# Byte offsets for the operands of the two MLP layers: weights at 0 modulo 128, activations at eight places

## The chip, the cores and the metric

The kernel runs on one core of a Trainium2 chip. The metric is the device time of one execution in microseconds (us). An engine here is one of PE (TensorE: matmuls, with its weight loads shown as PEld), DVE (VectorE), ACT (ScalarE), POOL (GpSimd) and SP (the queue that issues most DMAs). SBUF is the on-chip memory that the engines read: 128 partitions, and in each partition a row of bytes. A tile's place is the byte at which it begins in every partition.

## The reference

Causal attention, then two MLP layers, all in float32:

```
scores = q @ k^T / sqrt(64), masked above the diagonal      # 2 batches, 12 heads, 448 positions, 64 per head
attn   = softmax(scores) @ v                                # -> x: 896 tokens x 768
h      = max(x @ w_in, 0);      x = (h * h) @ w_out         # layer 1: 768 -> 2048 -> 768
h      = x @ w_in2;  out = (h - tanh(h)) @ w_out2           # layer 2: 768 -> 2048 -> 768
```

## The kernel before, in words

**Attention.** The twelve pairs of heads go through a pipeline (the loop over `s`, lines 579 to 669): scores, row maxima, exponentials, transposes, product with v. Into the gaps of the later pairs the first six products of the first MLP layer are put (`early`, line 510).

**MLP.** Each layer is done in two halves of 1024 hidden units (line 678). A half has two stages. `first` (line 498) makes eight groups for each of two batches: one group is one PSUM bank `h` of 128 x 448, summed over the six chunks of x. `second` (line 546) makes six groups for each batch: one bank `o`, summed over eight hidden chunks `g`. A product of float32 numbers is made of three matmuls on a rounded high part and a low part, written in `pieces` (line 411): high weights times high activations (L417), high times low (L418), low times high (L419). Each of them loads 128 x 128 weights (the stationary operand) and streams 448 columns (the moving operand). That makes 18 matmuls in a group of `first`, 24 in one of `second`, 288 in a stage, and 2304 in all over eight stages.

**Tiles.** A chunk of x (line 90; in layer 2 it is named y, line 563) is one tile of [high or low][batch][448]. Two hidden chunks share one tile of g, [high or low][2][448], in one of eight slots; line 488 chooses the slot: batch 0 uses slots 5, 6, 0, 1 and batch 1 slots 3, 2, 4, 7, in this order. A weight unit, 768 high and 768 low numbers, lies in one of eight ring tiles (line 168). The strides inside the tiles (1792 and 3584 bytes for activations, 512 and 3072 for weights) are all multiples of 128, so every operand of a tile begins at the same place modulo 128 as the tile itself.

**Places before.** The pool puts one tile behind the other. From the built program's allocation, modulo 128 bytes: all chunks of x begin at 32, all ring tiles at 96, slots 0, 1, 2 and 7 at 64, and slots 3, 4, 5 and 6 at 96.

**Order.** The order of all work is written out in the program and fixed; weights are unpacked by DVE and ACT (lines 123 to 158) between the activations, and nothing in the MLP stages waits for a planner.

Of the kernel before, what the change touches and what calls it, by code (L numbers as in the profile page):

```python
# [9 lines left out]
F32R = mybir.dt.float32r  # L10
# [9 lines left out]
B, H, S, D = 2, 12, 448, 64  # L20
DM = H * D
DFF = 2048
P = 128
KD = DM // P
# [3 lines left out]
NPAIR = B * NP  # L28
NQ = S // D
RING = 8  # L30
UNIT = 6
UC = UNIT * P
NU = 2 * (KF + DFF * DM // (P * UC))
# [48 lines left out]
def body(ctx: ExitStack, tc: tile.TileContext, qT, kT, vL, w1, w2, w3, w4, out):  # L82
    nc = tc.nc
    sb = ctx.enter_context(tc.tile_pool(name="sb", bufs=1))
# [2 lines left out]
    ident = sb.tile([P, P], F32, name="ident")  # L87
    mask = sb.tile([P, BEFORE + S], F32, name="mask")
    abias = sb.tile([P, 1], F32, name="abias")
    x = [sb.tile([P, 2, B, S], F32R, tag=f"x{k}", name=f"x{k}") for k in range(KD)]  # L90

    def slot(i, shape, dt, name):
        return sb.tile(shape, dt, tag=f"slot{i}", name=name)
# [29 lines left out]
    def w_prep(u):  # L123
# [8 lines left out]
        def merge():  # L132
            late()
            lo, hi = st["lo"], st["hi"]
            nc.vector.scalar_tensor_tensor(out=lo, in0=hi, scalar=3, in1=lo, op0=ALU.logical_shift_left, op1=ALU.bitwise_or)  # L135
            if u >= WOVEN:
                st["w"] = ring(u)
                act_late.append(lambda: nc.scalar.copy(out=st["w"][:, 0], in_=lo.bitcast(F32)))  # L138

        def high():  # L140
            st["w"] = ring(u)
            nc.vector.tensor_copy(out=st["w"][:, 0], in_=st["lo"].bitcast(F32))
# [22 lines left out]

    def ring(u):
        taken.append(u)
        return sb.tile([P, 2, UC], F32R, tag="w", bufs=RING, name=f"w{u}")

    def room():  # L170
        i = len(taken) - RING
        return i < 0 or taken[i] < freed[0]
# [10 lines left out]
    def late():  # L183
        while act_late:
            act_late.pop(0)()

    def one():

        if todo and budget[0] > 0 and (room() or not todo[0][3]):
            take()  # L190
            return True
# [64 lines left out]
    def hbank(name):  # L256
        n = hcount[0] % 8
        hcount[0] += 1
        tag, bufs = ("s", 4) if n < 4 else ("t", 2) if n < 6 else ("oh"[n - 6], 1)
        return ps.tile([P, 512], F32, tag=tag, bufs=bufs, name=name)[:, :S]  # L260
# [147 lines left out]
    g = {}  # L408
# [13 lines left out]
    def group(*args):  # L422
        for _ in pieces(*args):
            pass

    def hi_of(dst, v):
        nc.scalar.copy(out=dst[0], in_=v)  # L427

    def lo_of(dst, v):
        nc.vector.tensor_sub(out=dst[1], in0=v, in1=dst[0])  # L430
# [52 lines left out]
    gt = {}  # L483

    def gdst(l, half, m, b):

        if m % 2 == 0:
            i = (5, 6, 0, 1, 3, 2, 4, 7)[4 * b + m // 2]
            gt[b, m // 2] = slot(i, [P, 2, 2, S], F32R, f"g{l}_{half}_{b}_{m // 2}")
        t = gt[b, m // 2]  # L490
        g[m, b] = (t[:, 0, m % 2], t[:, 1, m % 2])
        return g[m, b]
# [5 lines left out]
    def first(l, half, m, b):  # L498

        u = (2 * l + half) * 2 * HALF + m  # L500
        dst = gdst(l, half, m, b)
        h = hbank(f"h{u}_{b}")
        for _ in first_pieces(l, half, m, b, h):
            pass
        if b == 1:
            freed[0] = u + 1
        return lambda: (act1, act2)[l](h, dst)


    def early(count):  # L510
        for m in range(count):
            dst = gdst(0, 0, m, 0)
            h = ps.tile([P, 512], F32, tag="h", bufs=1, name=f"h{m}_0")[:, :S]
            for k, _ in enumerate(first_pieces(0, 0, m, 0, h)):
                if k == KD - 1:
                    done.append((h, dst))
                yield
# [28 lines left out]
    def second(l, half, m, b):  # L546
        u0 = (2 * l + half) * 2 * HALF + HALF
        o = hbank(f"o{u0}_{m}_{b}")
        group(o, lambda k: (u0 + (m * HALF + k) // UNIT, (m * HALF + k) % UNIT), HALF, lambda k: g[k, b])
        if b == 1:  # L550
            freed[0] = u0 + (m + 1) * HALF // UNIT
        if half == 0:
            if b == 0 and m % 3 == 0:
                t = sb.tile([P, 3, B, S], F32, tag=f"v{m // 3}", name=f"part{l}_{m}")
                for i in range(3):
                    part[m + i] = t[:, i]
            nc.scalar.copy(out=part[m][:, b], in_=o)  # L557
        else:
            p = part[m][:, b]
            if l == 0:  # L560
                nc.vector.tensor_add(out=p, in0=o, in1=p)
                if b == 0:
                    x[m] = sb.tile([P, 2, B, S], F32R, tag=f"x{m}", name=f"y{m}")
                hi_of((x[m][:, 0, b], x[m][:, 1, b]), p)
                late()
                one()
                lo_of((x[m][:, 0, b], x[m][:, 1, b]), p)
            else:

                cuts = 2 if (m, b) == (KD - 1, B - 1) else 1  # L570
                w = S // cuts
                for i in range(cuts):
                    c = slice(i * w, i * w + w)
                    nc.vector.tensor_add(out=p[:, c], in0=o[:, c], in1=p[:, c])
                    (nc.scalar if i < cuts - 1 else nc.sync).dma_start(out=out[m * P : m * P + P, b * S + i * w : b * S + i * w + w], in_=p[:, c])
# [3 lines left out]
    for s in range(NPAIR + 2):  # L579
        p, a = s - 1, s - 2  # L580
        ss, sp, sa = s < NPAIR, 0 <= p < NPAIR, a >= 0
        f = s - 2 >= NP
# [95 lines left out]
    for l in range(2):  # L678
        for half in range(2):
            order = [(m, b) for m in range(HALF) for b in range(B)]  # L680
            if l == 0 and half == 0:
                order = [(EARLY, 0), *((m, 1) for m in range(EARLY + 1)), *order[2 * EARLY + 2 :]]
            for m, b in order:
                budget[0] = min(budget[0], 0) + (SHARE_HIDDEN[l] if l == 1 or m < HALF - 1 else 0)
                first(l, half, m, b)()
                pump()
            flush()
            for m in range(KD):
                for b in range(B):
                    budget[0] = min(budget[0], 0) + SHARE_OUT  # L690
                    second(l, half, m, b)
                    late()
                    pump()
# [42 lines left out]
```

## Time and profile before

| | us |
|---|---|
| median of 3 runs | 548.28 (548.06 to 548.43) |
| the profiled execution | 548.39 |
| its span in the profile | 546.6 |
| PE busy in the span | 538.0 (98%) |
| DVE, ACT busy | 345.8, 327.9 |

The profiled execution lasts 1.8 us longer than its span, which begins with the first and ends with the last instruction recorded. Matmuls are pipelined: one lasts some 0.36 us in the trace, but the next begins about 0.20 us after it. So the busy time of a matmul says little; the distance from one start to the next says what a matmul costs.

### The profile page before, as it was taken

Reading aid. Unit: us, or ns where it says so; the run is one execution under the profiler, and the core shown is the slowest. Engines: PE = TensorE matmul, PEld = TensorE weight load, DVE = VectorE, ACT = ScalarE, POOL = GpSimd, SP = SyncE. Lnnn points to the kernel's source line nnn. Section 1 sums busy time; section 2 is a strip of 40 time slices with the busy share of each in tenths; the row PEclk is TensorE's granted clock in tenths of the full one; section 3 lists DMA queues with packets and bytes.
Section 4 is the critical chain, followed back from the end, with each engine's and each line's share of the span. In section 5 each row is a group of like instructions: output and inputs, shape, how many; then the busy total and the mean of one; then the engine's idle time right before and its main releaser. Section 6 shows DMA issues by size and latency. Waiting matters only on the chain.

```text
span 546.6 us, 8248 instructions
## 1 busy us (share of the span) xinstructions
PE 538.0 (98%) x3206; PEld 483.6 (88%) x3206; DVE 345.8 (63%) x730; ACT 327.9 (60%) x630; POOL 4.2 (1%) x21
## 2 busy tenths in 40 slices
PE   8999999999999999999999999999999999999997
PEld 4668888899999999999999999999999999999996
DVE  5999998464624154444554688997654588887311
ACT  5999987577424266665232388776543687854100
POOL 1000000000000000000000000000000000000000
PEclk9999999999999999999999999999999999999999
DMA  8744323253433333331324130113655301026111
GB/s 296 268 150 131 113 80 106 105 174 115 163 128 116 115 117 116 115 116 58 116 83 149 58 117 1 59 58 113 231 176 174 113 5 58 1 71 212 50 52 50
DMA packets 15526, 61.86 MB, mean 113 GB/s; under 512 B 1664, under 2 KB 6400, under 8 KB 15488
## 3 DMA queue, kind: packets, MB, share of 16 engines
q1 hardware_dynamic: 15200, 61.00, 33.1%
q8 instruction: 25, 0.41, 0.3%
q10 hardware_dynamic: 288, 0.34, 0.2%
q14 instruction: 13, 0.11, 0.1%
HBM read 58.59 MB, written 2.75 MB: 112 GB/s over the span
## 4 chain that ended last, share of the span: by engine, by line
PE 92%; ACT 4%; DVE 3%; issue 0%; DVEq 0%; POOLq 0%; ACTq 0%
PE o L419 14%; PE o L418 14%; PE o L417 14%; PE h L417 14%; PE h L419 14%; PE h L418 14%; PE o L369 3%; ACT p L322 2%; PE t L357 2%; PE s L289 2%; DVE p L304 1%; DVE p L343 1%; ACT pt L364 1%; PE warm L238 1%; ACT raw L121 0%; DVE x L405 0%
## 5 line engine op out<-in xcount | busy, mean ns | idle before, releaser
L419 PE MATMUL o<-g,w 128*128 128x448 f32 x384 | 140.9, 367 | 0.0
L418 PE MATMUL o<-g,w 128*128 128x448 f32 x384 | 140.7, 366 | 0.0
L417 PE MATMUL o<-g,w 128*128 128x448 f32 x384 | 140.6, 366 | 0.0
L418 PEld LDWEIGHTS o<-g,w 128*128 128x128 f32 x384 | 72.1, 188 | 6.5
L419 PEld LDWEIGHTS o<-g,w 128*128 128x128 f32 x384 | 72.1, 188 | 6.4
L417 PEld LDWEIGHTS o<-g,w 128*128 128x128 f32 x384 | 72.1, 188 | 6.3
L417 PE MATMUL h<-x,w 128*128 128x448 f32 x192 | 71.5, 372 | 0.0
L417 PE MATMUL h<-y,w 128*128 128x448 f32 x192 | 69.7, 363 | 0.0
L419 PE MATMUL h<-y,w 128*128 128x448 f32 x192 | 69.6, 362 | 0.0
L419 PE MATMUL h<-x,w 128*128 128x448 f32 x192 | 69.5, 362 | 0.0
L418 PE MATMUL h<-x,w 128*128 128x448 f32 x192 | 69.4, 362 | 0.0
L418 PE MATMUL h<-y,w 128*128 128x448 f32 x192 | 69.1, 360 | 0.0
L138 ACT CAST w<-raw 128x768 fp32r<-128x768 f32 x56 | 50.4, 900 | 26.7 <-DVE raw L135 26.7
L135 DVE SCALAR_TENSOR_TENSOR raw<-raw 128x768 int32<-128x768 int32 x64 | 61.0, 953 | 5.4 <-ACT raw L121 5.4
L121 ACT ACTIVATE raw<-raw 128x768 f32<-128x768 f32 x64 | 58.8, 918 | 0.0
L151 DVE TENSOR_TENSOR w<-raw,w 128x768 fp32r<-128x768 f32 x32 | 30.6, 956 | 35.1 <-ACT w L138 35.0
L430 DVE TENSOR_TENSOR g<-r,g 128x448 fp32r<-128x448 f32 x32 | 20.0, 625 | 44.8 <-ACT g L427 44.7
L557 ACT COPY part<-o 128x448 f32<-128x448 f32 x24 | 12.8, 534 | 57.8 <-PE o L419 57.8
L149 DVE SCALAR_TENSOR_TENSOR w<-w,raw 128x768 fp32r<-128x768 f32 x32 | 30.6, 956 | 24.1 <-ACT w L138 24.0
L322 ACT ACTIVATE p<-p,st 128x256 f32<-128x256 f32 (+6 forms) x84 | 40.8, 513 | 4.3 <-DVE st L304 4.3
L419 PEld LDWEIGHTS h<-y,w 128*128 128x128 f32 x192 | 36.0, 188 | 2.8
L419 PEld LDWEIGHTS h<-x,w 128*128 128x128 f32 x192 | 36.0, 188 | 2.7
(57 smaller groups left out, 725.0 us busy)
## 6 DMA issues: line engine op xcount, KB each, us to landing
raw<-w SPq DMA_DIRECT2D x64, 768.0 KB, 4.3
q<-qT SPq DMA_DIRECT2D x12, 224.0 KB, 4.8
k<-kT SPq DMA_DIRECT2D x11, 224.0 KB, 3.7
out<-part SPq DMA_DIRECT2D x11, 224.0 KB, 1.9
v<-vL SPq DMA_DIRECT2D x2, 1152.0 KB, 6.6
vend<-vL SPq DMA_DIRECT2D x1, 384.0 KB, 8.3
k<-kT ACTq DMA_DIRECT2D x1, 224.0 KB, 3.5
out<-part ACTq DMA_DIRECT2D x1, 112.0 KB, 1.7
```

Source lines behind the costliest of these rows:

```text
L121: nc.scalar.activation(h, h, AF.Prelu, scale=2.0**-112, alpha=2.0**32)
L135: nc.vector.scalar_tensor_tensor(out=lo, in0=hi, scalar=3, in1=lo, op0=ALU.logical_shift_left, op1=ALU.bitwise_or)
L138: act_late.append(lambda: nc.scalar.copy(out=st["w"][:, 0], in_=lo.bitcast(F32)))
L149: nc.vector.scalar_tensor_tensor(out=w[:, 1], in0=w[:, 0].bitcast(F32), scalar=-(1.0 - 2.0**-24), in1=f, op0=ALU.mult, op1=ALU.add)
L151: nc.vector.tensor_sub(out=w[:, 1], in0=f, in1=w[:, 0])
L322: nc.scalar.activation(p, p, AF.Exp, bias=st[:, 0, i : i + 1], scale=-1.0, **kw)
L369: return nc.tensor.matmul(ob[n][D * j : D * j + D, o], lhsT=vs[b][kc][rows, D * h : D * h + D], rhs=rhs, skip_group_check=True, **flags).ins
L417: nc.tensor.matmul(h, lhsT=hi, rhs=xh, start=(k == 0), stop=False)
L418: nc.tensor.matmul(h, lhsT=hi, rhs=xl, start=False, stop=False)
L419: nc.tensor.matmul(h, lhsT=lo, rhs=xh, start=False, stop=(k == kk - 1))
L430: nc.vector.tensor_sub(out=dst[1], in0=v, in1=dst[0])
L557: nc.scalar.copy(out=part[m][:, b], in_=o)
```

## The change

Ring tiles, chunks of x and tiles of g are made 32 numbers (128 bytes) longer, and the kernel uses a view that begins a chosen number of elements inside. `X_AT`, `G_AT` and `W_AT` are those numbers in units of 4 bytes.

```
+LINE = 32
+X_AT = (8, 24, 0, 16, 28, 12)
+G_AT = (16, 20, 24, 20, 24, 28, 0, 12)
+W_AT = 8
...
-    x = [sb.tile([P, 2, B, S], F32R, tag=f"x{k}", name=f"x{k}") for k in range(KD)]
+    def shifted(shape, off, name, **kw):
+        n = shape[0] * shape[1] * shape[2]
+        t = sb.tile([P, n + LINE], F32R, name=name, **kw)
+        return t[:, off : off + n].rearrange("p (a b c) -> p a b c", a=shape[0], b=shape[1])
+    def x_tile(k, name):
+        return shifted((2, B, S), X_AT[k], name, tag=f"x{k}")
+    x = [x_tile(k, f"x{k}") for k in range(KD)]
...
-        return sb.tile([P, 2, UC], F32R, tag="w", bufs=RING, name=f"w{u}")
+        return shifted((1, 2, UC), W_AT, f"w{u}", tag="w", bufs=RING)[:, 0]
...
-            gt[b, m // 2] = slot(i, [P, 2, 2, S], F32R, f"g{l}_{half}_{b}_{m // 2}")
+            gt[b, m // 2] = shifted((2, 2, S), G_AT[i], f"g{l}_{half}_{b}_{m // 2}", tag=f"slot{i}")
...
-                    x[m] = sb.tile([P, 2, B, S], F32R, tag=f"x{m}", name=f"y{m}")
+                    x[m] = x_tile(m, f"y{m}")
```

The allocation of the changed program gives these places, modulo 128 bytes:

| operand | before | after |
|---|---|---|
| weights (ring tiles) | 96 | 0 |
| chunks 0 to 5 of x | 32 each | 64, 0, 32, 96, 16, 80 |
| slots 5, 6, 0, 1 of g (batch 0) | 96, 96, 64, 64 | 80, 96, 0, 16 |
| slots 3, 2, 4, 7 of g (batch 1) | 96, 64, 96, 64 | 48, 32, 64, 112 |

The instructions, their order on each engine and what each waits for are the same in both programs; only the addresses and the line numbers differ.

## Rows read from the trace of the kernel before

**Rows 1.** The page, part 1: busy us (share), instructions of each engine.

```profile
PE 538.0 (98%) x3206; PEld 483.6 (88%) x3206; DVE 345.8 (63%) x730; ACT 327.9 (60%) x630; POOL 4.2 (1%) x21
```

**Rows 2.** The page, part 4: the chain that ended last, by engine.

```profile
PE 92%; ACT 4%; DVE 3%; issue 0%; DVEq 0%; POOLq 0%; ACTq 0%
```

**Rows 3.** Waits of PE over the span: us, times, longest.

```profile
PE t L357 <- DVE p L343: 1.6, 2, 1.5
PE t L357 <- ACT pt L364: 1.3, 2, 0.7
PE o L369 <- DVE x L405: 0.9, 2, 0.4
```

**Rows 4.** Eight MLP stages in turn, PE alone: length, busy, matmuls, clock, DMA.

```profile
98.75:134.86 36.11, 36.11 (x185) 1.00 0.37 120
134.86:193.75 58.89, 58.89 (x289) 1.00 0.37 121
193.75:251.37 57.62, 57.62 (x290) 1.00 0.37 123
251.37:310.20 58.83, 58.83 (x289) 1.00 0.29 95
310.20:367.81 57.61, 57.61 (x289) 1.00 0.16 55
367.81:426.65 58.84, 58.84 (x290) 1.00 0.48 162
426.65:484.26 57.61, 57.61 (x289) 1.00 0.16 55
484.26:542.88 58.62, 58.62 (x288) 1.00 0.24 84
```

**Rows 5.** Timeline of a second stage: start, us, engine, line (slots 5, 0, 3, 2, 4, 7).

```profile
377.61 0.37 PE L417 MATMUL o<-g,w 128*128 128x448 f32 x1
...
380.05 0.37 PE L417 MATMUL o<-g,w 128*128 128x448 f32 x1
...
382.52 0.36 PE L417 MATMUL o<-g,w 128*128 128x448 f32 x1
382.71 0.36 PE L418 MATMUL o<-g,w 128*128 128x448 f32 x1
382.91 0.37 PE L419 MATMUL o<-g,w 128*128 128x448 f32 x1
...
383.73 0.37 PE L417 MATMUL o<-g,w 128*128 128x448 f32 x1
...
384.96 0.37 PE L417 MATMUL o<-g,w 128*128 128x448 f32 x1
...
386.19 0.37 PE L417 MATMUL o<-g,w 128*128 128x448 f32 x1
...
387.42 0.37 PE L417 MATMUL o<-g,w 128*128 128x448 f32 x1
```

**Rows 6.** Timeline in the attention part: bf16 matmuls on one constant.

```profile
8.40 1.13 PE L238 MATMUL warm<-const-bfloat16-1.0 128*128 128x448 bf16 x5
```

**Rows 7.** The same line grouped: ns min/median/max, first and last start.

```profile
L238 PE MATMUL warm<-const-bfloat16-1.0 x14: 353/577/577, 0.8 to 9.2; 128*128 128x448 bf16 x14
```

**Rows 8.** The page, part 5: weight loads; busy us, mean ns, idle before.

```profile
L418 PEld LDWEIGHTS o<-g,w 128*128 128x128 f32 x384 | 72.1, 188 | 6.5
...
L419 PEld LDWEIGHTS h<-y,w 128*128 128x128 f32 x192 | 36.0, 188 | 2.8
```

**Rows 9.** Timeline of a first stage: weights of the next matmul load under each.

```profile
340.21 0.36 PE L417 MATMUL h<-y,w 128*128 128x448 f32 x1
340.22 0.19 PEld L418 LDWEIGHTS h<-y,w 128*128 128x128 f32 x1
...
340.41 0.36 PE L418 MATMUL h<-y,w 128*128 128x448 f32 x1
340.42 0.19 PEld L419 LDWEIGHTS h<-y,w 128*128 128x128 f32 x1
```

## The prediction

> **What bounds the kernel now.** I read the page's busy shares first: PE is busy for 98% of the span, DVE and ACT for about 60% [rows 1]. Then the chain that ended last: 92% of it is PE [rows 2]. The waits of PE come to a few microseconds, all on attention lines (L357, L369), none on a matmul of the MLP [rows 3]. So for the MLP the question is not who is waited for, but how far apart PE starts its own matmuls.
>
> The table by stage answers that [rows 4]. The window edges are the starts of the stages' first matmuls, and a whole stage has 288 (the one or two more that a row counts run in over its edges). A `first` stage takes 57.61 / 288 = 200.0 ns per matmul, a `second` stage 58.84 / 288 = 204.3 ns. Both have the same shape, 128 x 128 against 128 x 448. The granted clock is 1.00 in all eight rows, the 2.4 GHz level. The DMA share goes from 0.16 to 0.48, and the distance does not follow it: the two `first` stages at 0.16 and the one at 0.37 agree to 0.01 us. That speaks against memory traffic as the reason and leaves the operands themselves.
>
> Inside a `second` stage the distance changes where the tile changes [rows 5]. The twelve matmuls from 377.61 read slots 5 and 6, place 96: 2.44 / 12 = 203.3 ns. The twelve from 380.05 read slots 0 and 1, place 64: 2.47 / 12 = 205.8. Then come sixes: slot 3 (96) 1.21 / 6 = 201.7, slot 2 (64) 1.23 / 6 = 205.0, slot 4 (96) 1.23 / 6 = 205.0, slot 7 (64) 205.0. Over all 24 of each place that is 4.88 / 24 = 203.3 ns at 96 and 4.93 / 24 = 205.4 at 64. Chunks of x, at 32, run at 200.0. The weights lie at 96 throughout. So a dependence on place is there before anything is changed, and it is 5 ns wide. Slots 3 and 4 share a place and differ by 3.3 ns, so what ran just before matters as well, by about as much.
>
> How much could be had at all? Five bf16 matmuls of the same 448 columns, all reading one constant, take 1.13 us from the first start to the last end [rows 6]; taking off the shortest single duration of 0.353 [rows 7] leaves 0.78 over four distances: 194 ns. Three matmuls on slot 3, from 382.52 to 382.91, are 195 ns apart [rows 5]. So 195 ns is the least that the trace shows for a real operand.
>
> **The change part by part.** No instruction is added, removed or moved, and no wait changes. The extra 128 bytes per tile are not read or written by anything. What is left is the distance of 2304 matmuls, of which 108 run in the gaps of attention, where PE waits for others; they count for nothing here. That leaves 1044 of `first` and 1152 of `second`.
>
> What the three known places have in common is the weights at 96. I take the difference of places, moving minus weights modulo 128, as the variable: 64 gives 200.0 ns (x), 0 gives 203.3 (slots at 96), 96 gives 205.4 (slots at 64). One wave round the circle through these three has the mean (200.0 + 203.3) / 2 = 201.65, and by it 32 would give 197.9. After the change the differences are 64, 0, 32, 96, 16, 80 for x and all eight multiples of 16 for g. Over either set the wave's ups and downs cancel, so both kinds of stage come to 201.65. Straight lines between the three points instead of a wave give a mean of 202.5 for both sets (the differences in between: 16 gives 202.5, 32 gives 201.7, 48 gives 200.8, 80 gives 202.7, 112 gives 204.4).
>
> - x gets worse: (201.65 - 200.0) x 1044 = +1.7 us (straight lines: +2.6).
> - g gets better: (201.65 - 204.3) x 1152 = -3.1 us (straight lines: -2.1).
> - Switching place between neighbours happens at 147 of the 2303 steps before and at 571 after. The sixes after a switch ran at 201.7 and 205.0 on the same place [rows 5], on either side of the 203.3 of that place, so a switch has no sign that I can read; I take 0. A switch could be worth up to 1.7 ns on each of the 424 new ones, +-0.7 us.
> - Weights at 0 instead of 96: no fp32r weights at another place are in the trace. All their loads last 188 ns [rows 8] and begin 0.01 us after the matmul before [rows 9], so the load ends about 12 ns before the next start, whichever operand streams. If the place of the weights by itself cost nothing, 0; if it made what separates 200 ns from the 195 of the best rows, -5 ns on 2196 or -11 us; in the other direction a step as wide as that from x to the slots at 64, +5.4 ns, would be +11.9. I take 0, since the load's 188 ns is the same in both kinds of stage, and keep the ends.
>
> The sum is 1.7 - 3.1 = -1.4 us on the profiled execution of 548.39, which is 546.6 of span and 1.8 around it: 547.0. The median of the runs is 0.1 lower, so 546.9. With straight lines it would be +0.5, or 548.8; the wave is my choice because the measured points turn by 5 ns within 32 bytes, which corners would not do. This one case reaches from 545 to 549.5.
>
> A rule speaks against any change. The Trainium skill (SBUF — State Buffer, "Who interferes with whom") gives PE two independent read ports, one for the moving operand and one for weights, and says that PE never waits on another engine. By that page the place of an operand would cost nothing. The trace does not agree as it stands, since equal matmuls at equal clock take 200.0 and 204.3 ns. Also by the skill (TensorE: Matmul & The Clock Gate, "Back-to-back issue gap") 448 columns would be 189 ns apart (an estimate from its formula), and no stage here reaches that; what lies above it is what places could give back.
>
> **The rivals.**
>
> - *Most of the stall goes* (0.18). The weights on a full 128-byte line, or neighbours at different places, remove the collision. Then all matmuls come to about the 196 ns of the best rows: (200.0 - 196) x 1044 + (204.3 - 196) x 1152 = 4.2 + 9.6 = 13.8 us less, 534.5. For it: 195 ns was reached right after a switch from 64 to 96. Against it: four of every six steps in x, and five of every six in g, still have no switch, and the next switch (slot 2 to slot 4) shows nothing of the kind.
> - *Places do not matter* (0.16). The 200 and 204 could belong to something else in which the stages differ, such as the lengths of their groups (18 and 24) or the step from one accumulation to the next. Then the time stays at 548.3. It would also stay if only bytes below the 16-byte step count, since all places before and after are multiples of 16. Against it: within one `second` stage the distance moves with the slot.
> - *x loses its good place* (0.30). The chunks of x all sit at the best difference that the trace shows, opposite to the weights, and run at 200.0 without a single longer distance. In the changed kernel five of six chunks leave it. If they go to the 204.3 of the present `second` stages and g, spread over good and bad, gains nothing, the cost is 4.3 x 1044 = 4.5 us: 552.8. It decides the sign as soon as x loses more than 3.1 / 1044 = 3.0 ns where g gains its 3.1 us. For it: two of the three known differences lie above 203. Against it: g has nowhere worse to go that the trace shows.
>
> **How the numbers follow.** The forecast has 0.36, the rivals 0.18, 0.16 and 0.30. A difference under 0.2%, 1.1 us, is not told from none: 547.2 to 549.4 counts as the same. Of the forecast I put about 0.26 on faster, 0.06 on the same and 0.04 on slower; of the first rival all 0.18 on faster, with what is left of small gains in the others at 0.04; no effect gives 0.14 to the same; the loss of x's place 0.28 to slower. Together 0.48 faster, 0.20 the same, 0.32 slower. The likeliest case gives 546.9. The range goes from 534.5, where the first rival lies, to 552.8, where the third does.
>
> **What would show it.** The table by stage of the changed kernel: `first` near 58.1 us and `second` near 58.1 as well would bear out the wave. `first` still at 57.6 and `second` at 58.8 would mean that places do not matter. Both near 56.5 would be the first rival; `first` at 58.9 the third. The timeline within one group of x should show six different paces, one for each chunk, the chunk at 32 the fastest and the one at 96 the slowest. If the paces do not order by the difference of places, the variable is wrong even where the sum is right. The distance from a load's start to its matmul's start shows whether the weights' own place has a price.

## The result, and the profile after

The changed kernel takes 550.98 us (median of 4, 550.15 to 551.64) where the kernel before takes 548.36 (548.06 to 548.44): a ratio of 1.0051, 95% interval 1.0037 to 1.0065. It is slower by 2.6 us. The forecast was 546.9, a gain of 1.4; its range, 534.5 to 552.8, holds the time, but the sign is wrong.

The page of the changed kernel, busy shares and chain, answers to [rows 1, 2]:

```profile
span 549.2 us, 8248 instructions
PE 540.8 (98%) x3206; PEld 484.5 (88%) x3206; DVE 346.2 (63%) x730; ACT 327.8 (60%) x630; POOL 4.1 (1%) x21
...
PE 92%; ACT 4%; DVE 3%; DMA 1%; issue 0%; DVEq 0%; POOLq 0%; ACTq 0%
```

The same instructions, the same chain but for 1% of DMA, and PE busy 2.8 us longer. The waits of PE stand where they stood [rows 3], on attention lines alone (us, times, longest):

```profile
PE t L371 <- DVE p L357: 1.6, 2, 1.5
PE t L371 <- ACT pt L378: 1.0, 2, 0.6
PE o L383 <- DVE x L419: 0.9, 2, 0.4
```

So the time went into the pace, the distance from one matmul's start to the next, and the table of the eight MLP stages (length, PE busy, matmuls, clock, DMA share, GB/s) shows in which:

```profile
98.97:135.62 36.65, 36.65 (x185) 1.00 0.35 121
135.62:194.28 58.66, 58.66 (x290) 1.00 0.36 122
194.28:252.76 58.48, 58.48 (x289) 1.00 0.37 122
252.76:311.43 58.67, 58.67 (x290) 1.00 0.29 95
311.43:369.91 58.48, 58.48 (x289) 1.00 0.17 55
369.91:428.57 58.66, 58.66 (x289) 1.00 0.50 162
428.57:487.06 58.49, 58.49 (x290) 1.00 0.17 54
487.06:545.51 58.45, 58.45 (x289) 1.00 0.24 84
```

Against [rows 4]: the four `first` stages take 212.1 us where they took 208.9 (58.48 / 288 = 203.1 ns a matmul, was 200.0); the four `second` stages 234.4 where they took 235.2 (203.7 ns, was 204.3). That is +3.2 - 0.8 = +2.4 us of the 2.6 that the span grew. The clock is 1.00 in every row, as before.

A stretch of a `first` stage of the changed kernel (start, duration, engine, line) shows the pace change from chunk to chunk, which it did not before [rows 9]:

```profile
330.93 0.36 PE L431 MATMUL h<-y,w 128*128 128x448 f32 x1
...
331.53 0.37 PE L431 MATMUL h<-y,w 128*128 128x448 f32 x1
...
332.15 0.37 PE L431 MATMUL h<-y,w 128*128 128x448 f32 x1
...
332.75 0.37 PE L431 MATMUL h<-y,w 128*128 128x448 f32 x1
...
333.37 0.37 PE L431 MATMUL h<-y,w 128*128 128x448 f32 x1
```

Three matmuls each: 0.60 us at place 32, 0.62 at 96, 0.60 at 16, 0.62 at 80. The same chunk does not take the same time in the next group. By the starts of all matmuls in the eight stages, without the very first, the mean paces of the chunks are 202.3 (64), 202.3 (0), 201.4 (32), 205.3 (96), 203.5 (16) and 203.5 ns (80).

### The profile page after: what moved, and what is told of

It reads as the page before. It is cut to its first block, busy times and chain, and to the rows that moved or that the text cites. A ratio compares the mean times of both kernels' runs of the same rounds, so it can differ in the third digit from the quotient of the medians.

```text
span 549.2 us, 8248 instructions
## 1 busy us (share of the span) xinstructions
PE 540.8 (98%) x3206; PEld 484.5 (88%) x3206; DVE 346.2 (63%) x730; ACT 327.8 (60%) x630; POOL 4.1 (1%) x21
## 4 chain that ended last, share of the span: by engine, by line
PE 92%; ACT 4%; DVE 3%; DMA 1%; issue 0%; DVEq 0%; POOLq 0%; ACTq 0%
PE h L431 14%; PE o L431 14%; PE o L433 14%; PE o L432 14%; PE h L432 14%; PE h L433 14%; PE o L383 3%; ACT p L336 2%; PE t L371 2%; PE s L303 2%; DVE p L318 1%; DVE p L357 1%; ACT pt L378 1%; DMA k<-kT 1%; ACT raw L135 0%; DVE x L419 0%
## 5 line engine op out<-in xcount | busy, mean ns | idle before, releaser
L431 PEld LDWEIGHTS h<-x,w 128*128 128x128 f32 x192 | 36.2, 188 | 3.1
L433 PEld LDWEIGHTS h<-x,w 128*128 128x128 f32 x192 | 36.1, 188 | 3.0
```

The lines of the kernel that those rows point to most:

```text
L431: nc.tensor.matmul(h, lhsT=hi, rhs=xh, start=(k == 0), stop=False)
L433: nc.tensor.matmul(h, lhsT=lo, rhs=xh, start=False, stop=(k == kk - 1))
```

## The experiments

"Place" is where an operand begins, modulo 128 in the first round and modulo 256 from then on. All timed runs had the kernel before beside them on the same chip. The weights are at 0 unless said otherwise.

### Round 1: which part, and is it the difference to the weights?

The theories: D, the difference between the moving operand and the weights sets the pace, as the prediction assumed; P, the moving operand's absolute place does; S, steps from one place to another cost. Edits to the changed kernel, here and below the new lines alone:

```
# shift_all: everything 32 bytes on, so all differences are those of before
+X_AT = (8, 8, 8, 8, 8, 8)
+G_AT = (8, 8, 8, 8, 8, 8, 8, 8)
# x64_gspread: the change for g alone
+X_AT = (8, 8, 8, 8, 8, 8)
# xspread_gbefore: the change for x alone
+G_AT = (8, 8, 8, 8, 8, 8, 8, 8)
# uniform64: x and g all at 64
+X_AT = (8, 8, 8, 8, 8, 8)
+G_AT = (0, 0, 0, 24, 24, 24, 24, 0)
```

> Every MLP tile moved by the same 32 bytes: weights at 0, all chunks of x at 64, slots of g at 96 and 0, so every difference (moving minus weights, modulo 128) is what it was before the change. Theory D (the difference decides the pace): as before, first stages 57.6 us, second stages 58.8, about 548.4. Theory P (the absolute place of the moving operand decides; 32 gave 200.0 ns, 96 gave 203.3, 64 gave 205.4): x at 64 goes to 205.4, first stages 59.2 us, and the time rises by about 5 us to 553. Theory S (only a change of place between neighbours costs): as before, 548.4.

> The change done for g alone: weights at 0, all chunks of x at 64 (their difference of before), g at its eight places as in the changed kernel. D and S: first stages back at 57.6 us, second stages as in the changed kernel at 58.4 to 58.7, so 547.7 to 548.2. P: x at 64 loses as well, first stages above 58.5, 551 or more.

> The change done for x alone: weights at 0, x at its six places as in the changed kernel, g at 96 and 0 (its differences of before). D and S: first stages 58.5 us as in the changed kernel, second stages 58.8, so 551 to 551.7, the whole of the loss and a little more. If x is not what lost, 548.4.

> Weights at 0, all chunks of x and all slots of g at 64: one difference, 64, everywhere. D: every stage at 200.0 ns, second stages 57.6 us, 548.4 - 4 x 1.2 = 543.5. P: as slots at 64 were, 205 ns everywhere, 554. Kind of stage (x and g differ by the length of their groups, not by place): first 57.6, second 58.8, 548.4.

| kernel | us | ratio (95%) | first, second stage, ns a matmul |
|---|---|---|---|
| shift_all | 550.55 | 1.0039 (1.0024 to 1.0055) | 202.8, 203.9 |
| x64_gspread | 550.10 | 1.0035 (1.0017 to 1.0053) | 202.7, 203.7 |
| xspread_gbefore | 550.95 | 1.0045 (1.0030 to 1.0059) | 203.1, 203.8 |
| uniform64 | 547.86 | 0.9991 (0.9976 to 1.0005) | 202.8, 201.7 |

This upset all three theories. With every difference modulo 128 as before, `shift_all` lost nearly as much as the change did, and x at 64 throughout, without a step modulo 128, ran at 202.8 ns where D and S both wanted 200.0. P wanted 205. Undoing either half of the change gave back at most 0.4 ns a matmul (`first`, 203.1 to 202.7). What these four share with the changed kernel is the tiles' greater length: 7168 and 6144 bytes are multiples of 256, 7296 and 6272 are not, so neighbouring tiles, alike modulo 128, differ by 128 modulo 256.

### Round 2: the length of the tiles

Theory L: what must be alike is the place modulo 256. From `u64_256` on all runs have `LINE = 64` and `W_AT = 40`, shown or not.

```
# pad_only: longer tiles, no offsets
+X_AT = (0, 0, 0, 0, 0, 0)
+G_AT = (0, 0, 0, 0, 0, 0, 0, 0)
+W_AT = 0
# plain_shift32: the kernel before, all of it 32 bytes on
+    sb.tile([P, 8], F32, name="spacer")
# u64_256: 256 bytes longer, x and g at 64
+LINE = 64
+X_AT = (40, 40, 40, 40, 40, 40)
+G_AT = (32, 32, 32, 56, 56, 56, 56, 32)
+W_AT = 40
# u32_256: the same with x and g at 32
+X_AT = (32, 32, 32, 32, 32, 32)
+G_AT = (24, 24, 24, 48, 48, 48, 48, 24)
```

> Only the 128 extra bytes per tile, no chosen offset: modulo 128 every operand begins where it began before (weights 96, x 32, g 96 and 64), but neighbouring tiles now differ by 128 modulo 256. In the kernel before all chunks of x, and all ring tiles, begin alike modulo 256 too. Theory L (the pace needs equal places modulo 256, and the longer tiles break it): first stages 58.4 us as when all tiles were moved by 32 bytes (202.8 ns), 550.5. Theory P (the absolute place modulo 128): as before, first stages 57.6, 548.1.

> The kernel before with an unused spacer of 32 bytes ahead of x: all operands move by 32 bytes, tile lengths as before. L: as before, first 57.6 us, second 58.8, 548.1. P: first stages 58.4 us, second 58.7, 550.5, as when the same places were reached with longer tiles.

> Tiles longer by 256 bytes in place of 128, weights at 0 and all x and g at 64, now modulo 256. L with the difference as the variable: 200.0 ns in all eight stages, second stages 57.6 us, 548.1 - 4.9 = 543.2. P: as with 64 modulo 128, first 58.4, second 58.1, 547.9.

> The same with all x and g at 32 modulo 256, weights at 0. By the wave of the prediction 197.9 ns everywhere, second and first stages 57.0 us, about 538.5. If only the locked difference of 64 is good, 203 ns everywhere, about 549.

`pad_only` took 550.77 us (1.0046, 1.0031 to 1.0061), `plain_shift32` 548.00 (0.9999, 0.9989 to 1.0008). Two rows of each, a `first` and a `second` stage; `pad_only`:

```profile
311.20:369.60 58.40, 58.40 (x289) 1.00 0.16 55
369.60:428.32 58.72, 58.72 (x289) 1.00 0.48 162
```

and `plain_shift32`:

```profile
310.30:367.91 57.61, 57.61 (x290) 1.00 0.16 55
367.91:426.74 58.83, 58.83 (x289) 1.00 0.47 162
```

Moving everything by 32 bytes changes nothing, to 0.01 us a stage; 128 unread bytes in each tile cost the `first` stages 0.8 us each. The absolute place is out, as far as one move of 32 bytes shows, and L holds so far. Then `u64_256`, 543.07 us (0.9908, 0.9893 to 0.9923):

```profile
307.69:365.29 57.60, 57.60 (x289) 1.00 0.16 55
365.29:422.89 57.60, 57.60 (x289) 1.00 0.49 165
422.89:480.49 57.60, 57.60 (x289) 1.00 0.16 55
```

Both kinds of stage take 57.60 / 288 = 200.0 ns. So the 204.3 of the `second` stages before [rows 4] belonged to their slots' places and not to the kind of stage. `u32_256` gave 543.17 us (0.9909, 0.9890 to 0.9929):

```profile
307.51:365.11 57.60, 57.60 (x289) 1.00 0.16 55
365.11:422.71 57.60, 57.60 (x289) 1.00 0.48 165
```

That is 200.0 as well, not the 197.9 of the prediction's wave: no stage of any run came below 200.0.

### Round 3: places or steps?

```
# spread_256: the changed kernel's places, tiles 256 bytes longer
+LINE = 64
+X_AT = (40, 24, 32, 48, 28, 44)
+G_AT = (16, 20, 24, 52, 56, 60, 0, 44)
# u0_256: x and g at 0
+X_AT = (24, 24, 24, 24, 24, 24)
+G_AT = (16, 16, 16, 40, 40, 40, 40, 16)
# alt_act128: x and g at 64 and 192 in turn
+X_AT = (40, 8, 40, 8, 40, 8)
+G_AT = (32, 0, 0, 56, 56, 56, 24, 0)
# alt_w128: u64_256 with ring tiles at 128 and 0 in turn
+        return shifted((1, 2, UC), W_AT % 32, f"w{u}", line=32, tag="w", bufs=RING)[:, 0]
```

> The changed kernel's places (weights 0, x at 64, 0, 32, 96, 16, 80, g at eight multiples of 16), but with tiles longer by 256 bytes, so that they hold modulo 256. Theory L (a stage runs at 200.0 ns where all operands of a kind begin alike modulo 256, and any step from one place to another costs): no better than the changed kernel, 203 to 204 ns in all stages, 550 to 551. Theory H (only steps of 128, which the longer tiles brought, cost): 200 to 201 ns, 543 to 545.

> Weights, x and g all at 0 modulo 256. L: 200.0 ns in all stages, 543.1, as at 64 and at 32. D (the difference between moving operand and weights has its own pace; 0 ran at 203.3 in the kernel before): 203.3 ns, 550.

> As the kernel with 64 modulo 256 everywhere, but the chunks of x and the tiles of g are at 64 and 192 in turn; weights all at 0. L and H: 202 to 203 ns in first stages (a step every third matmul), 201.5 in second (every sixth), 546 to 548. If the weights' alternation was what the longer tiles spoiled: 200.0, 543.1.

> As the kernel with 64 modulo 256 everywhere, but neighbouring ring tiles are at 128 and 0 in turn, so the weights step by 128 once per group of first. If only steps of the moving operand cost: 200.0 ns, 543.1. If the difference to the weights must hold: half of the time at another pace, 201 to 202 ns, 545 to 547.

| kernel | us | ratio (95%) | first, second stage, ns |
|---|---|---|---|
| spread_256 | 550.42 | 1.0040 (1.0025 to 1.0055) | 203.0, 203.7 |
| u0_256 | 549.02 | 1.0014 (1.0004 to 1.0023) | 202.7, 202.7 |
| alt_act128 | 548.57 | 1.0007 (0.9998 to 1.0017) | 202.8, 202.2 |
| alt_w128 | 545.58 | 0.9952 (0.9937 to 0.9967) | 201.2, 201.3 |

A `first` and a `second` stage of `spread_256`:

```profile
310.65:369.12 58.47, 58.47 (x289) 1.00 0.16 55
369.12:427.80 58.68, 58.68 (x290) 1.00 0.47 162
```

and of `u0_256`:

```profile
309.94:368.31 58.37, 58.37 (x290) 1.00 0.16 55
368.31:426.67 58.36, 58.36 (x289) 1.00 0.47 163
```

`spread_256` runs like the changed kernel, so for spread operands the length of the tiles is not the reason. `u0_256` went against L: all alike, and yet 202.7 in both kinds of stage. A place therefore has a pace of its own after all. `alt_w128` bears this out from the other side: its activations all stay at 64, only the weights alternate, and the matmuls whose difference is 64 ran at 200.1 to 200.3 ns, those at 192 (64 less 128, modulo 256) at 202.3 to 202.4. Round 4 gives 202.2 for 192 reached by moving x. It is the difference, modulo 256 and not 128.

### Round 4: the pace of each place, and a step without a change of pace

All x at one place and all g at another, in five runs.

```
# x16_g48
+X_AT = (28, 28, 28, 28, 28, 28)
+G_AT = (28, 28, 28, 52, 52, 52, 52, 28)
# x80_g112
+X_AT = (44, 44, 44, 44, 44, 44)
+G_AT = (44, 44, 44, 4, 4, 4, 4, 44)
# x128_g160
+X_AT = (56, 56, 56, 56, 56, 56)
+G_AT = (56, 56, 56, 16, 16, 16, 16, 56)
# x192_g224
+X_AT = (8, 8, 8, 8, 8, 8)
+G_AT = (8, 8, 8, 32, 32, 32, 32, 8)
# x96_g144
+X_AT = (48, 48, 48, 48, 48, 48)
+G_AT = (52, 52, 52, 12, 12, 12, 12, 52)
```

> Weights at 0, all x at 16, all g at 48, modulo 256. Theory D (each difference to the weights, modulo 256, has its own pace; 0 gave 202.7, 32 and 64 gave 200.0): x between 200.0 and 203, g at 200.0; 543 to 546. Theory S (steps cost, places but a few do not): 200.0 in both, 543.1.

> Weights at 0, all x at 80, all g at 112. D: near 96, which gave 205.6 in the kernel before, so x 202 to 204 and g 203 to 206; 550 to 553. S: 200.0 in both, 543.1.

> Weights at 0, all x at 128, all g at 160. If the period of the paces were 128 bytes, as 0 and 32: x 202.7, g 200.0, 546. D with period 256: other values, 200 to 206.

> Weights at 0, all x at 192, all g at 224. With period 128, as 64 and 96: x 200.0, g 205.6, 550. D with period 256, from the run with alternating weights, where the matmuls at 192 ran at 202.4: x 202.4 to 203, g unknown, 546 to 552.

> Weights at 0, all x at 96, all g at 144. From the slots at that difference in the kernel before, x at 205.6 or a little more; g at 144 not known, 200 to 206. 548 to 557. If x came to 203 or less, the mean of the places would fall to 201.5 and the steps would be worth 1.5 ns instead of 1.1.

A `first` and a `second` stage of `x80_g112` (554.32 us; 1.0117, 1.0101 to 1.0133):

```profile
313.11:371.67 58.56, 58.56 (x289) 1.00 0.16 55
371.67:431.19 59.52, 59.52 (x290) 1.00 0.48 160
```

of `x16_g48` (546.75 us; 0.9977, 0.9968 to 0.9987):

```profile
309.04:366.64 57.60, 57.60 (x290) 1.00 0.16 55
366.64:425.09 58.45, 58.45 (x289) 1.00 0.48 163
```

and of `x96_g144` (556.46 us; 1.0152, 1.0137 to 1.0167):

```profile
313.85:372.99 59.14, 59.14 (x290) 1.00 0.17 54
372.99:432.50 59.51, 59.51 (x290) 1.00 0.49 160
```

A `first` stage of `x128_g160` (547.33 us; 0.9987, 0.9977 to 0.9996) and one of `x192_g224` (550.49 us; 1.0046, 1.0031 to 1.0062):

```profile
309.65:368.41 58.76, 58.76 (x290) 1.00 0.17 54
311.05:369.29 58.24, 58.24 (x290) 1.00 0.16 55
```

A row's length over 288 is the pace of a place used alone. Places 0, 32 and 64 were used alone in both kinds of stage and gave the same pace in both; the others were used in one kind only. All together, ns:

| 0 | 16 | 32 | 48 | 64 | 80 | 96 | 112 | 128 | 144 | 160 | 192 | 224 |
|---|---|---|---|---|---|---|---|---|---|---|---|---|
| 202.7 | 200.0 | 200.0 | 203.0 | 200.0 | 203.3 | 205.3 | 206.7 | 204.0 | 206.6 | 200.0 | 202.2 | 204.4 |

The upper half does not repeat the lower (0 and 128, 64 and 192). This is no wave: four of thirteen places lie on a floor of 200.0, and the others above it by up to 6.7. Nor can a place be told from its neighbours: 48, between two places on the floor, was expected at 200.0 and took 203.0.

Last, a step between two places that both lie on the floor:

```
# alt_32_64: x and g at 32 and 64 in turn
+X_AT = (32, 40, 32, 40, 32, 40)
+G_AT = (24, 32, 32, 48, 48, 48, 56, 32)
```

> Weights at 0; chunks of x and tiles of g at 32 and 64 in turn, modulo 256, two places that run at 200.0 ns each by themselves. If the paces of places are all: 200.0 in all stages, 543.1. If a step costs what the mixed kernel suggests (1.1 ns per matmul where every third, or every sixth, is followed by a step): first 201.1, second 201.1, 545.5.

It took 550.18 us (1.0037, 1.0023 to 1.0051), three times the loss that was expected of a step. Its timeline in a `first` stage, from a chunk at 32 to one at 64 and back:

```profile
320.05 0.37 PE L431 MATMUL h<-y,w 128*128 128x448 f32 x1
320.26 0.37 PE L432 MATMUL h<-y,w 128*128 128x448 f32 x1
320.46 0.37 PE L433 MATMUL h<-y,w 128*128 128x448 f32 x1
320.67 0.36 PE L431 MATMUL h<-y,w 128*128 128x448 f32 x1
320.87 0.36 PE L432 MATMUL h<-y,w 128*128 128x448 f32 x1
321.07 0.36 PE L433 MATMUL h<-y,w 128*128 128x448 f32 x1
321.27 0.37 PE L431 MATMUL h<-y,w 128*128 128x448 f32 x1
```

The chunk at 32 takes 0.62 us for its three, 206.7 ns each; the chunk at 64 takes 0.60, 200.0 each; and so it goes on through the stage. The place that ran at 200.0 alone runs at 206.7 beside the other, while 64 loses nothing. So the step itself is not paid once: it leaves the operand behind it in a slower rhythm of the same place. In the `second` stages all six matmuls of a tile at 32 run at 206.7.

Nor does the neighbour alone decide which rhythm it is. The first MLP stage, 180 matmuls with the same two places in turn, is faster than the same kind of stage later:

```profile
98.32:134.62 36.30, 36.30 (x184) 1.00 0.35 120
310.29:368.85 58.56, 58.56 (x289) 1.00 0.16 55
```

That is 201.7 ns a matmul against 203.3. By the starts in the first row the chunk at 32 takes 0.607 us for its three there, 202.5 ns each. One place thus shows three paces, 200.0, 202.5 and 206.7, and what chooses between the last two is open.

## Why the prediction was wrong

- **The bound was right.** PE's own distance from start to start carried the whole result; no wait and no other engine moved.
- **The variable, "moving minus weights modulo 128".** This step failed. `pad_only` kept every difference modulo 128, and every switch between them, and took 2.6 us more: its x stands at 64 and 192 in turn, two places with paces of their own (200.0 and 202.2 ns) and a step of 128 between them. In the changed kernel the longer ring tiles begin at 0 and at 128 modulo 256 in turn (by the allocation of the built program). So each chunk of x meets the weights at the place in the table of the change for half of its matmuls, and 128 further on for the other half: twelve differences, not six, and sixteen for g. The extra bytes are indeed "not read or written by anything", and they still matter: they move the next tile.
- **x gets worse, +1.7 us.** Right in sign. Eleven of the twelve differences have a pace in the table, with a mean of 202.6 ns, so places alone make (202.6 - 200.0) x 1044 = +2.7 us, an estimate.
- **g gets better, -3.1 us.** Right in sign, too large. Thirteen of the sixteen differences have a pace in the table; weighted by their matmuls the mean is 202.7, so (202.7 - 204.3) x 1152 = -1.8 us, an estimate.
- **Switching place, "I take 0".** This step failed too. The stages run at 203.1 and 203.7 ns, 0.5 and 1.0 above those means: 0.5 x 1044 + 1.0 x 1152 = +1.7 us, where the bound was 0.7 either way. The differences that were not run leave it between +0.5 and +2.4, if they lie between 200.0 and 206.7. `spread_256`, with the weights all at 0, shows the term by itself: the six and the eight places have means of 201.9 and 202.6, and its stages run 1.1 above each, 1.1 x 1044 + 1.1 x 1152 = +2.4 us. A switch has no fixed price: by the same working the term goes from -0.1 ns a matmul (`second` of `shift_all`) to +3.3 (`alt_32_64`). The two sixes and the twelve in [rows 5] at place 96 showed that a place has more than one pace; that was written down as noise between two signs.
- **The sum.** 2.7 - 1.8 + 1.7 = +2.6 us, which is, but for rounding, the +2.4 of the eight stages. Of the 4.0 us between -1.4 and +2.6 the variable makes 2.3 and the switches 1.7. This split is bookkeeping: `alt_32_64` shows that pace and step are not independent, and a run without any new step modulo 128 (`pad_only`, 550.77 us) and one without the differences of 128 (`spread_256`, 550.42) each lose about what the change lost.
- **Weights at 0, "I take 0".** Right for the place modulo 128: `plain_shift32` moved the weights from 96 to 0 with everything else, and the stages did not change by 0.02 us.
- **The signs.** Of the six chunks the one at 32 is the fastest and the one at 96 the slowest, as foretold. But the paces do not follow the wave: 64 is at 202.3 where it had 200.0, and a chunk's pace changes from group to group.
- **The rivals.** The loss of x's good place came true in part (+3.0 ns on x, but g gained 0.6 as well). That places do not matter is refuted: equal matmuls with other engines equally busy run between 200.0 and 206.7 ns by place alone. This pace depends on where the moving operand lies relative to the weights, which the two independent read ports of PE in the Trainium skill (SBUF — State Buffer, "Who interferes with whom") do not lead one to expect; that PE waits on no other engine is not touched by it. The great gain did not come from spreading but lay the other way: all operands of a kind at one good place. The 196 ns of the first rival is not there: the 195 of [rows 5] was two short distances within a six of 1.21 us, and at the floor too (`u64_256`) single distances go from 197 to 202 ns.
- **Two small readings.** The straight lines have a mean of 202.6, not 202.5, which makes them +0.7 us and not +0.5. And the 189 ns comes from a formula that the Trainium skill (TensorE: Matmul & The Clock Gate, "Back-to-back issue gap") gives for an isolated matmul, not for a stream with weight loads.

What the floor of 200.0 ns is made of, why the period is 256 bytes, and by which rule a step leaves a place in its slow rhythm, is not settled. How the loss of the changed kernel divides between places and switches is known only as estimated above. No run went under 200.0, and no run varied places finer than 16 bytes or gave the high and low parts different places.

## What to carry to other kernels

Where PE follows itself without waits, read its pace stage by stage and tile by tile from start to start: more than 2% can lie in where tiles begin (543.07 to 556.46 us here). Try all moving operands at one place relative to the weights modulo 256, with tile lengths that are multiples of 256, padding included; then measure which place. Here 64 for all gave 543.07 us against 548.13 beside it, 0.9% for a spare 256 bytes a tile, while the spread places, and 128 bytes of padding by themselves, each cost 0.5%. All this is shown for one form of matmul only.

## What the runs showed of the hardware that was not expected

The float32r matmul of 448 columns with a weight load for each, its operands all at one place, has a pace that goes by (moving place - weights' place) modulo 256: 200.0 ns at 16, 32, 64 and 160, up to 206.7 at 112. With two places in turn the same place can hold other paces: 32 runs at 200.0 alone, and at 202.5 or 206.7 beside 64. Moving both operands together by 32 bytes changes nothing (548.00 against 548.13 us).
